# A hand-written order of all queues replaced by another, with eight PSUM banks in one pool

## The chip, the cores and the metric

The kernel runs on one core of a Trainium2 chip. The metric is device microseconds for one execution; before the change the median of three runs was 536.09 us (535.41 to 536.63). A core has five engines, each with its own queue of instructions that it works off in order: TensorE (PE in the profile, with its weight loads as PEld), VectorE (DVE), ScalarE (ACT), GpSimd (POOL) and SyncE (SP), which here issues all DMAs. Engines wait for each other through semaphores. Matmuls write to PSUM, which has eight banks; the other data lie in SBUF, and inputs and outputs in HBM.

## The reference

Two blocks follow each other. The first is a gated linear attention with a state that decays step by step; the second is an MLP with a hard-swish between its two matrices.

```python
# q, k, v, alpha: (B=4, H=8, S=768, D=48)
for t in range(S):
    state = alpha[:, :, t, :, None] * state + einsum('bhd,bhe->bhde', k[:, :, t], v[:, :, t])
    y[:, :, t] = einsum('bhd,bhde->bhe', q[:, :, t], state)
x = y.transpose(0, 2, 1, 3).reshape(3072, 384)
h = x @ w_in                              # (384, 2048)
g = h * clip(h + 3, 0, 6) / 6
out = g @ w_out                           # (2048, 384) -> (3072, 384)
```

The two weight matrices arrive as 64-bit floats and are turned into 32-bit ones on the chip. All else is 32-bit.

## The kernel before

**Attention in chunks.** The 4 x 768 tokens are cut into 24 chunks of 128 (numbered j). For a chunk, alpha, k, q and v are loaded (steps `la`, `lk`, `lq`, `lv`). For the first six chunks alpha, k and q lie in a ring of three buffers (`rings`) and are transposed by TensorE (`ta`, `tk`, `tq`, line 282); from the seventh on they are loaded in blocks and transposed by VectorE (line 286). VectorE then scans alpha backwards (`r`, line 309) and forwards (`p`, line 320) and multiplies k and q by the results (`k`, `q`, line 332). TensorE makes the scores in two halves (`sc`, line 346), which VectorE masks (`m`, line 356). k goes back to token order, by TensorE and a ScalarE copy (`kb`, `ck`, lines 374 and 378) in the first eight chunks, later by a VectorE transpose and a round trip through DRAM (`kt`, `kw`, `kr`, lines 391 to 404). TensorE makes the state update (`u`, line 429), VectorE adds it to the state (`sm`, lines 437 and 439), GpSimd decays it (`st`, line 409), and ScalarE places the state (`sv`, line 419) and q (`qa`, line 366) where the output matmuls read them. TensorE makes the chunk's output (`ya`, `yb`, line 455) and ScalarE copies it as x of the MLP (`cy`, line 464).

**Weights in slices.** There are 16 slices of 768 KB: 0 to 7 of `w_in`, 8 to 15 of `w_out`. Each is loaded (`w`, lines 162 and 166) and made 32-bit by ScalarE (`d2` line 196, `d1` line 186, for some slices `dx` line 191), VectorE (`d3`, lines 203 to 210) and, last, a GpSimd addition (`d4`, line 217).

**The MLP in groups.** A group g is two chunks, 256 tokens, so there are twelve. Groups 0 and 1 use plain matmuls for the first matrix: `fa` and `fb` (line 489) for half a group, `f` (line 478) for a whole one; the numbers after the name are the group, the slice of the weights and a bank. Group 0 uses them for the second matrix too (`b`, line 516). All other products go by schemes that need fewer matmuls and more additions: for the first matrix, 20 products `M` of four matmuls each (line 600) with sums of x (`xc`), sums of weights (`y`), copies (`n`, line 606) and output sums (`o`), where most additions are lines 537 to 541; for the second, seven products `P` of eight matmuls (line 703) with sums of the activations (`s`, lines 647 and 664), of the weights (`x`, line 647), copies (`K`, line 682) and output sums (`G`, lines 716 and 719), and a store (`O`, line 724). The activation is a ScalarE step (`fr`, `e`, line 494) and a VectorE step (`fg`, `h`, line 498). A 32-bit matmul shows as two passes in the profile (x8 is four matmuls), a transpose as one.

**Banks.** `banks` holds four PSUM tiles, t0 to t3, for attention; `bank_m` holds four others, m0 to m3, for the MLP. A step that starts a result in PSUM names its bank by a number: `sc.2.0.2` puts the two halves of the scores of chunk 2 into t0 and t2, `M.2.7.0` starts a sum of products in m0. A bank that is written again waits for its last reader.

**The order.** Nothing is planned when the kernel is built: one string lists all 1788 steps, and each step issues its instructions on its engines in that order, so the string sets all five queues. The list begins with idle matmuls (`z`, line 532, 29 in all: `z.0.5` is five of them in bank m0) mixed with the first loads.

Of the kernel before, what the change touches and what calls it, by code (L numbers as in the profile page):

```python
# [17 lines left out]
def kernel(  # L18
# [42 lines left out]
    G = 2  # L61
# [161 lines left out]
    banks = [ps.tile([C, NP * C], FP, tag=f"t{i}", name=f"t{i}_ps") for i in range(4)]  # L223
# [246 lines left out]
    bank_m = [ps.tile([C, GT * 2], FP, tag=f"m{i}", name=f"m{i}_ps") for i in range(4)]  # L470

# [278 lines left out]
    with tc.manual_schedule():  # L750
        run("""z.0.5 z.0.3 z.0.1 z.0.8 qa.0.0 w.0 d2.0 d3.0 la.0 ta.0.0 ca.0 r.0 lk.0 tk.0.1 k.0
               z.0.2 p.0 la.1 ta.1.2 lq.0 tq.0.3 ca.1 r.1 lk.1 lv.0.0 sv.0.0 d1.0 kb.0.0 ck.0 z.0.2
               u.0.2.1 sm.0.0 sv.0.1 q.0 qa.0.1 tk.1.0 k.1 p.1 z.0.2 sc.0.2.3 m.0 la.2 ta.2.0 ca.2
               dx.0 w.2 d2.2 kb.1.0 ck.1 lq.1 r.2 sm.0.1 st.1 tq.1.2 q.1 d3.2 z.0.3 d1.2 dx.2 lv.1.1
               u.1.3.1 sv.1.0 sm.1.0 p.2 sm.1.1 sc.1.0.2 m.1 ya.0.3 yb.0 cy.0 lq.2 w.1 d1.1 tq.2.1
               q.2 d4.2 lk.2 tk.2.3 k.2 fa.2.0 d4.0 st.2 sc.2.0.2 d2.1 d3.1 m.2 dx.1 d4.1 qa.1.1
               lk.3 la.3 ta.3.1 ca.3 la.4 fa.0.1 sv.1.1 w.3 r.3 ta.4.3 ca.4 r.4 tk.3.1 k.3 kb.2.0
               qa.1.0 d2.3 ya.1.2 yb.1 cy.1 fa.1.2 lq.3 ck.2 d1.3 p.3 d3.3 lv.2.2 u.2.3.2 sm.2.0
               d4.3 fb.2 tq.3.1 q.3 fb.1 qa.2.0 sm.2.1 sv.2.0 st.3 fr.0.2.0 fg.0.2 lk.4 tk.4.0
               sv.2.1 w.5 d2.5 k.4 d3.5 d1.5 qa.3.0 d4.5 qa.2.1 sc.3.1.3 m.3 w.6 d2.6 d1.6 d3.6 d4.6  # L760
               lv.3.0 lq.4 w.7 kb.3.2 fb.0 f.0.3.3 kb.4.0 ya.2.1 ck.3 u.3.3.2 sm.3.0 fr.0.3.1 fg.0.3
               fr.0.1.0 fg.0.1 qa.3.1 sv.3.0 sm.3.1 p.4 d2.7 sv.3.1 d1.7 d3.7 d4.7 f.0.5.0 fr.0.5.1
               fr.0.0.0 fg.0.5 fg.0.0 tq.4.3 ck.4 la.5 ta.5.2 f.0.6.3 ca.5 w.4 d2.4 ya.3.0 yb.3 cy.3
               fr.0.6.1 yb.2 cy.2 w.9 d2.9 q.4 qa.4.1 d1.4 d1.9 dx.4 la.6 w.8 d3.4 r.5 lk.5 w.10
               d3.9 p.5 ca.6 fg.0.6 d4.9 w.12 lq.5 lv.4.1 d2.8 d3.8 f.0.7.2 d1.8 st.4 d4.8 d4.4 w.11
               fr.0.7.0 fg.0.7 f.1.7.0 fr.1.7.1 fg.1.7 sc.4.0.2 m.4 f.1.1.1 fr.1.1.0 fg.1.1 f.1.3.3
               fr.1.3.1 d2.10 d1.10 tk.5.3 f.1.0.2 d2.12 d3.10 d4.10 w.13 fg.1.3 fr.1.0.0 fg.1.0 k.5
               d3.12 lq.6 f.1.6.0 f.1.2.1 u.4.1.0 sm.4.0 d1.12 d4.12 sv.4.0 qa.4.0 ya.4.2 fr.1.6.1
               fg.1.6 w.15 tq.5.3 fa.4.3 sv.4.1 d2.11 kb.5.1 d2.13 fr.1.2.0 f.1.4.2 fr.1.4.1 d1.11
               sm.4.1 q.5 r.6 d3.11 d3.13 fg.1.4 d4.11 lv.5.0 lk.6 tq.6 p.6 d2.15 d3.15 fg.1.2 d1.13  # L770
               d4.13 sc.5.0.3 yb.4 f.1.5.0 fr.1.5.1 fg.1.5 tk.6 m.5 b.1.0.2 fb.4 b.1.1 d1.15 d4.15
               st.5 y.5 w.14 la.7 lk.7 cy.4 d2.14 qa.5.1 ck.5 b.0.0.1 fr.0.4.0 d3.14 k.6 q.6 ca.7
               fg.0.4 d1.14 d4.14 x.0 y.1 y.10 b.0.1 y.0 y.2 u.5.2 P.1.0.0 K.1.0 qa.5.0 sv.5.0
               qa.6.1 P.1.1.3 b.0.2 b.1.2 kb.6.0 ya.5.3 y.6 s.1.0.0 sm.5.0 sv.5.1 G.1.0.0 tk.7
               s.1.1.1 s.1.2.3 x.1 yb.5 cy.5 b.1.3 sc.6.1.2 lv.6.2 ck.6 u.6.3.0 s.1.3.2 x.2 P.1.2
               b.0.3 K.1.1 y.7 s.1.4 s.1.5 y.11 y.3 r.7 xc.2.1 x.3 y.4 y.8 xc.2.3 k.7 xc.2.0 xc.2.4
               y.9 y.12 y.16 y.13 y.15 P.1.3.3 K.1.2 P.1.4 bo.1 P.1.5 xc.2.5 G.1.1.1 P.1.6 y.14 y.17
               y.19 xc.2.6 sm.6.0 G.1.2.2 y.20 M.2.0.2 lv.12.1 la.8 O.1.1 O.1.0 ca.8 y.18 y.21 y.23
               so.1 G.1.3.3 n.2.0.8 bo.0 lq.7 lv.7.0 O.1.2 m.6 xc.2.2 xc.2.10 xc.2.7 tq.7 r.8 p.7
               xc.2.8 sv.6.1 M.2.15.3 M.2.1 kb.7.3 n.2.1.9 M.2.16 M.2.2 n.2.2.10 M.2.7.0 n.2.7.11  # L780
               sm.6.1 xc.2.9 q.7 p.8 M.2.3 M.2.4 n.2.4.12 M.2.8 o.2.0.0 M.2.5 n.2.5.13 qa.7.0 sv.6.0
               st.7 lk.8 O.1.3 lq.8 lk.9 la.9 la.10 tk.8 tq.8 lq.10 lq.9 ya.6.1 yb.6 M.2.9 z.1.3
               M.2.18.1 o.2.1.0 e.2.1.1 M.2.10 cy.6 ck.7 sc.7.0.2 u.7.1.3 n.2.10.14 M.2.11 qa.7.1
               ca.9 la.11 y.22 M.2.6.2 h.2.1 q.8 m.7 e.2.0.0 h.2.0 n.2.11.15 qa.6.0 n.2.18.10 qa.8.1
               M.2.12 M.2.19 n.2.12.12 M.2.13 sm.7.0 sv.7.1 r.9 k.8 o.2.3.0 sv.7.0 ya.7.0 y.24
               o.2.5.0 n.2.13.12 o.2.2.0 yb.7 cy.7 sc.8.1.2 xc.3.1 o.2.2.1 e.2.2.1 xc.3.3 o.2.3.1
               M.2.14 xc.3.4 xc.3.0 xc.3.5 o.2.4.0 xc.3.7 xc.3.6 o.2.6.0 P.2.0.1 M.3.0.2 M.2.17
               h.2.2 o.2.6.1 e.2.3.0 h.2.3 o.2.7.0 K.2.0 n.3.0.12 M.3.1 n.3.1.9 e.2.5.1 M.3.7.0
               n.3.7.13 xc.3.8 o.2.7.1 xc.3.2 kt.8 e.2.6.0 h.2.6 tk.9 M.3.2 n.3.2.10 e.2.4.0 P.2.1.3
               h.2.4 h.2.5 s.2.0.14 e.2.7.0 G.2.0.1 h.2.7 M.3.3 M.3.4 n.3.4.8 k.9 s.2.1.11 M.3.8  # L790
               o.3.0.0 ca.10 kt.9 P.2.3.3 s.2.2.15 s.2.3.14 lv.8.2 kw.8 kr.8 lk.10 sm.7.1 xc.3.9
               M.3.5 n.3.5.11 K.2.2 e.3.0.1 xc.3.10 M.3.9 o.3.1.0 P.2.2 K.2.1 u.8.0.3 M.3.18.2 s.2.5
               M.3.10 n.3.10.14 n.3.18.15 e.3.1.0 s.2.4 P.2.4 tq.9 h.3.0 st.8 sv.8.0 M.3.11 n.3.11.8
               tk.10 p.9 sm.8.0 q.9 r.10 k.10 qa.9.0 qa.9.1 m.8 sm.8.1 h.3.1 M.3.19 o.3.5.0 kt.10
               P.2.5 G.2.2.0 st.9 M.3.12 sc.9.0.1 qa.8.0 n.3.12.10 o.3.3.0 kw.9 lv.9.0 kr.9 sv.8.1
               u.9.2.3 sm.9.0 sv.9.1 sv.9.0 G.2.1.2 sm.9.1 st.10 M.3.15.2 M.3.16 M.3.6.3 M.3.13 m.9
               o.3.4.0 o.3.6.0 tq.10 n.3.13.10 o.3.2.0 e.3.4.1 ya.8.2 yb.8 ya.9.3 yb.9 cy.9 M.3.14
               M.3.17 cy.8 xc.4.1 P.2.6 e.3.5.0 G.2.3.3 o.3.2.1 xc.4.3 h.3.4 xc.4.4 o.3.6.1 xc.4.5
               xc.4.0 xc.4.6 e.3.2.1 M.4.0.0 n.4.0.10 P.3.0.1 xc.4.7 o.3.7.0 p.10 h.3.5 o.3.3.1
               xc.4.8 M.4.7.3 M.4.1 xc.4.2 h.3.2 o.3.7.1 lk.11 O.2.2 tk.11 e.3.6.0 e.3.3.1 h.3.3  # L800
               P.3.1.2 e.3.7.1 n.4.1.13 M.4.2 K.3.0 ca.11 q.10 h.3.6 r.11 k.11 h.3.7 n.4.7.15
               lv.10.2 lv.11.0 kw.10 sc.10.0.1 kr.10 G.3.0.0 u.10.3.2 sm.10.0 qa.10.1 n.4.2.14 M.4.3
               M.4.4 M.4.8 s.3.0.9 xc.4.9 s.3.2.12 s.3.1.11 P.3.3.2 n.4.4.8 M.4.5 o.4.0.0 e.4.0.0
               sv.10.1 sm.10.1 xc.4.10 kt.11 O.2.0 O.2.3 lq.11 m.10 s.3.3.9 s.3.5 M.4.9 o.4.1.0
               P.3.2 sv.10.0 st.11 n.4.5.11 K.3.2 la.13 M.4.18.0 p.11 tq.11 lk.12 tk.12 K.3.1 M.4.10
               n.4.10.9 q.11 qa.10.0 n.4.18.12 e.4.1.1 la.12 s.3.4 ca.12 h.4.0 r.12 P.3.5 G.3.2.1
               h.4.1 M.4.11 P.3.4 n.4.11.8 M.4.12 n.4.12.14 qa.11.0 M.4.19 p.12 G.3.1.3 lq.12 kw.11
               O.2.1 tq.12 kr.11 u.11.3 sc.11.0.2 sv.11.0 O.3.1 lk.13 P.3.6 qa.11.1 M.4.6.2 G.3.3.2
               k.12 o.4.3.0 m.11 sm.11.0 sv.11.1 kt.12 M.4.13 n.4.13.14 q.12 o.4.3.1 e.4.3.0 o.4.2.0
               o.4.6.0 h.4.3 o.4.2.1 ya.10.1 ya.11.0 yb.10 yb.11 cy.11 cy.10 xc.5.1 ca.13 xc.5.3  # L810
               M.4.15.1 M.4.16 M.4.14 P.4.0.2 o.4.4.0 M.4.17 xc.5.4 o.4.5.0 xc.5.0 xc.5.5 M.5.0.0
               o.4.6.1 e.4.2.1 h.4.2 P.4.1.3 qa.12.1 e.4.4.0 xc.5.6 o.4.7.0 h.4.4 o.4.7.1 tk.13
               K.4.0 n.5.0.14 M.5.1 e.4.7.1 h.4.7 e.4.5.0 xc.5.2 h.4.5 xc.5.7 G.4.0.3 e.4.6.1 h.4.6
               s.4.1.12 s.4.0.11 xc.5.8 r.13 xc.5.9 xc.5.10 k.13 kw.12 kr.12 la.14 sc.12.2.3
               u.12.0.1 sm.12.0 n.5.1.13 M.5.2 n.5.2.15 M.5.7.1 n.5.7.8 P.4.3.3 s.4.2.9 kt.13 lk.14
               lq.13 O.3.0 O.3.3 lv.13.2 kw.13 O.4.0 lq.14 tq.13 lq.15 M.5.3 M.5.4 M.5.8 s.4.3.10
               P.4.2 sv.12.1 n.5.4.11 o.5.0.0 e.5.0.0 K.4.2 s.4.5 p.13 ca.14 M.5.9 M.5.5 n.5.5.12
               m.12 sm.12.1 o.5.1.0 q.13 P.4.5 K.4.1 G.4.2.0 qa.12.0 qa.18.0 s.4.4 h.5.0 M.5.18.0
               n.5.18.9 o.5.6.0 tk.14 qa.13.0 M.5.10 n.5.10.10 M.5.15.3 M.5.16 M.5.11 M.5.19 r.14
# [113 lines left out]
```

## Time and profile before

| What | Value |
|---|---|
| Median of three runs | 536.09 us |
| The profiled execution's span | 533.7 us |
| TensorE busy | 524.6 us, 6306 passes |
| VectorE busy | 477.2 us, 849 instructions |
| ScalarE busy | 257.2 us |
| GpSimd busy | 50.4 us, 71 instructions |
| DMA | 54.40 MB, mean 102 GB/s |
| Granted TensorE clock | 1.00 in all stages |

A row of the profile names the source line, the engine, the operation, the written tile and the tiles read, and a count. The chain of work that ended last follows the last instruction back to what released it, step by step; its rows have a start, a length and what ran. Most of it is TensorE (85%). A matmul's end is modelled in the profile, so a busy TensorE may still run slower than it could; how long a block of matmuls takes is read from the start of the next. The profiled execution's time is its span, 533.7 us, 2.4 below the median of the runs.

### The profile page before, as it was taken

To read this page: it belongs to the slowest core of one execution; us is meant where nothing else is said; L and a number is where in the kernel's file an instruction comes from. 1 tells how busy PE (TensorE), PEld (TensorE's weight loads), DVE (VectorE), ACT (ScalarE), POOL (GpSimd) and SP (SyncE) were. 2 spreads that over 40 slices of the span, in tenths; PEclk is the share of its full clock that TensorE was granted. 3 is DMA by queue.
4 is the path that set the end of the run, shared out by engine and by line. 5 is a ranking of instruction groups with operands and counts; after the bars stand their busy time and mean duration, and the time that the engine had idled before them with its cause. 6 is when DMAs were issued, how large, how long until landed. Compare 5 with 4: busy or idle time off the path is not lost.

```text
span 533.7 us, 15143 instructions
## 1 busy us (share of the span) xinstructions
PE 524.6 (98%) x6306; PEld 499.4 (94%) x6306; DVE 477.2 (89%) x849; ACT 257.2 (48%) x503; POOL 50.4 (9%) x71
## 2 busy tenths in 40 slices
PE   8799999999999999999999999999999999999997
PEld 7698886789999999999999999999999999999997
DVE  6999989999999999998999999999999899496382
ACT  3889865212653553553544444642634544553340
POOL 5333425100000000000000000000000000000000
DMA  9998876005615155254344355044454042100001
GB/s 174 217 252 256 215 216 152 21 2 154 152 30 116 32 121 135 57 140 95 87 110 113 91 124 140 19 120 102 115 136 104 11 110 43 44 2 2 15 16 37
DMA packets 124100, 54.40 MB, mean 102 GB/s; under 512 B 83328, under 2 KB 116864, under 8 KB 124032
## 3 DMA queue, kind: packets, MB, share of 16 engines
q1 hardware_dynamic: 124032, 53.44, 42.5%
q8 instruction: 49, 0.80, 0.6%
q14 instruction: 19, 0.16, 0.1%
HBM read 44.50 MB, written 8.91 MB: 100 GB/s over the span
## 4 chain that ended last, share of the span: by engine, by line
PE 85%; DVE 8%; POOL 2%; DMA 2%; ACT 1%; issue 1%; SPq 1%; DVEq 0%; POOLq 0%
PE m_ps L703 34%; PE m_ps L600 34%; PE m_ps L478 5%; PE t_ps L455 4%; PE t_ps L346 2%; PE t_ps L429 2%; PE m_ps L489 2%; PE t_ps L282 1%; DVE rings L647 1%; DMA v<-in_v_dram 1%; DVE raw L537 1%; ACT raw L191 1%; DMA kq<-in_k_dram 1%; DVE g_sb L647 1%; DVE w L537 1%
## 5 line engine op out<-in xcount | busy, mean ns | idle before, releaser
L606 ACT COPY g_sb<-m_ps 128x512 f32<-128x512 f32 x110 | 63.6, 584 | 124.9 <-PE m_ps L600 104.1
L703 PE MATMUL m_ps<-w,g_sb 128*128 128x192 f32 x704 | 121.7, 327 | 0.0
L703 PEld LDWEIGHTS m_ps<-w,g_sb 128*128 128x128 f32 x704 | 113.7, 190 | 0.4
L703 PE MATMUL m_ps<-rings,g_sb 128*128 128x192 f32 x528 | 91.5, 326 | 0.0
L703 PEld LDWEIGHTS m_ps<-rings,g_sb 128*128 128x128 f32 x528 | 85.4, 190 | 0.1
L600 PE MATMUL m_ps<-xc,w 128*128 128x128 f32 x640 | 82.7, 277 | 0.3 <-DVE w L541 0.3
L600 PEld LDWEIGHTS m_ps<-xc,w 128*128 128x128 f32 x640 | 77.5, 192 | 1.5 <-issue 0.5
L494 ACT ACTIVATE r<-g_sb,half 128x512 f32<-128x512 f32 x80 | 56.8, 722 | 32.9 <-DVE g_sb L541 12.1
L498 DVE SCALAR_TENSOR_TENSOR g_sb<-r,g_sb 128x512 f32<-128x512 f32 x80 | 53.6, 682 | 4.6 <-ACT r L494 4.2
L600 PE MATMUL m_ps<-xT,raw 128*128 128x128 f32 x400 | 52.5, 277 | 0.0
L600 PEld LDWEIGHTS m_ps<-xT,raw 128*128 128x128 f32 x400 | 48.6, 192 | 0.6
L409 POOL TENSOR_TENSOR st<-sm,R 128x192 f32<-128x192 f32 x20 | 12.9, 643 | 353.8 <-DVE sm L439 306.7
L647 DVE TENSOR_TENSOR g_sb<-g_sb 128x512 f32<-128x512 f32 (+1 forms) x55 | 42.0, 795 | 0.2
L600 PE MATMUL m_ps<-xT,w 128*128 128x128 f32 x320 | 42.0, 276 | 0.0
L600 PEld LDWEIGHTS m_ps<-xT,w 128*128 128x128 f32 x320 | 39.3, 192 | 0.1
L366 ACT COPY A<-q 48x256 f32<-48x256 f32 x88 | 35.5, 404 | 5.0 <-DVE q L332 3.7
L356 DVE TENSOR_TENSOR A<-t_ps,mask 64x256 f32<-64x256 f32 x96 | 36.0, 414 | 0.4
L478 PE MATMUL m_ps<-xT,w 128*128 128x256 f32 x144 | 32.8, 382 | 0.0
L600 PE MATMUL m_ps<-xc,raw 128*128 128x128 f32 x240 | 31.8, 276 | 0.0
L309 DVE TENSOR_TENSOR_SCAN R<-t,ones 128x516 f32<-128x516 f32 x24 | 29.7, 1236 | 1.1 <-ACT t L300 1.0
L478 PEld LDWEIGHTS m_ps<-xT,w 128*128 128x128 f32 x144 | 26.7, 190 | 3.6
L600 PEld LDWEIGHTS m_ps<-xc,raw 128*128 128x128 f32 x240 | 29.6, 192 | 0.1
(104 smaller groups left out, 731.0 us busy)
## 6 DMA issues: line engine op xcount, KB each, us to landing
raw<-in_moe_w_out_dram SPq DMA_DIRECT2D x8, 768.0 KB, 5.2
raw<-in_moe_w_in_dram SPq DMA_DIRECT2D x6, 768.0 KB, 6.8
v<-in_v_dram SPq DMA_DIRECT2D x48, 96.0 KB, 3.0
out_dram<-oh SPq DMA_DIRECT2D x44, 96.0 KB, 1.7
far<-kq SPq DMA_DIRECT2D x64, 64.0 KB, 2.2
kb<-far SPq DMA_DIRECT2D x64, 64.0 KB, 2.0
aq<-in_alpha_dram SPq DMA_DIRECT2D x36, 96.0 KB, 2.5
qq<-in_q_dram SPq DMA_DIRECT2D x36, 96.0 KB, 2.4
```

The lines of the kernel that those rows point to most:

```text
L309: nc.vector.tensor_tensor_scan(out=reverse(R, n - 1, n), data0=reverse(ax, n, n), data1=reverse(ones, n, n), initial=0.0, op0=ALU.mult, op ...
L356: nc.vector.tensor_tensor(out=to[:, a], in0=sc[a][half], in1=mask[half, half].unsqueeze(1).to_broadcast([HB, NP, HB]), op=ALU.mult)
L366: nc.scalar.copy(out=to[:, a], in_=Q_t[j][64 * a : 64 * a + D, :, half])
L409: nc.gpsimd.tensor_tensor(out=st, in0=sm, in1=R_t[j][:, :, 0:1].to_broadcast([C, NP, D]), op=ALU.mult)
L455: nc.tensor.matmul(y_of(j, (i + 1) // 2, p)[:, HB * b : HB * b + HB], vb[:, p, e : e + 32], A_t[j][:, b, 2 * p + a], start=(b == 0 and i = ...
L478: nc.tensor.matmul(h[:, f], w1[:, kk, o : o + C], xT_t[g][:, kk], start=(kk == 0), stop=(kk == KT - 1))
L494: nc.scalar.activation(out=to, in_=h, func=AF.Relu, bias=half, scale=1.0 / 6.0)
L498: nc.vector.scalar_tensor_tensor(out=to, in0=r, scalar=1.0, in1=h, op0=ALU.min, op1=ALU.mult)
L600: nc.tensor.matmul(acc[g][i][:, f * C : (f + 1) * C], spots[w][:, f * C : (f + 1) * C], x_of(g, x), start=(first and f == 0), stop=last, s ...
L606: nc.scalar.copy(out=slots[z], in_=acc[g][i])
L647: nc.vector.tensor_tensor(out=out, in0=in0, in1=in1, op=ALU.subtract)
L703: nc.tensor.matmul(to[g], a, rhs[:, f], start=(first and f == 0), stop=(last and f == HF - 1), skip_group_check=True)
```

## The change

It has two parts. One line joins the two lists of banks, so that attention's steps and the MLP's can each name any of the eight: numbers 0 to 3 are a step's own former four, 4 to 7 the other side's. And the string of steps is another one. It holds the same 1788 steps with the same counts of each kind; their order differs nearly everywhere, and so do the bank, buffer and slot numbers. What is computed and by which instruction is the same.

In the start, the first loads are those of alpha, k and q, and slice 2 of the weights is the first slice, behind v of the first chunk; before, slice 0 came first of all. The 29 idle matmuls are 8, 2, 2, 3, 1, 2, 5, 3 and 3 (before 5, 3, 1, 8, 2, 2, 2, 3 and 3). Later, the steps that hold attention's small matmuls (`sc`, `u`, `ya`, `yb`) stand next to each other more often.

```diff
     bank_m = [ps.tile([C, GT * 2], FP, tag=f"m{i}", name=f"m{i}_ps") for i in range(4)]
+    banks, bank_m = banks + bank_m, bank_m + banks
...
-        run("""z.0.5 z.0.3 z.0.1 z.0.8 qa.0.0 w.0 d2.0 d3.0 la.0 ta.0.0 ca.0 r.0 lk.0 tk.0.1 k.0
-               z.0.2 p.0 la.1 ta.1.2 lq.0 tq.0.3 ca.1 r.1 lk.1 lv.0.0 sv.0.0 d1.0 kb.0.0 ck.0 z.0.2
-               u.0.2.1 sm.0.0 sv.0.1 q.0 qa.0.1 tk.1.0 k.1 p.1 z.0.2 sc.0.2.3 m.0 la.2 ta.2.0 ca.2
...
+        run("""la.0 z.4.8 ta.0.1 ca.0 lk.0 r.0 z.1.2 tk.0.4 k.0 z.4.2 lq.0 tq.0.3 z.4.3 la.1 ta.1.4
+               p.0 lk.1 q.0 lv.0.2 w.2 z.5.1 kb.0.1 sc.0.6.5 lq.1 ca.1 tk.1.3 r.1 k.1 ck.0 u.0.7.1
+               sm.0.0 sm.0.1 z.3.2 kb.1.4 tq.1.2 la.2 m.0 qa.0.1 la.3 st.1 p.1 q.1 lv.1.0 sv.0.0
+               ya.0.3 sv.0.1 d2.2 w.1 yb.0 d1.2 dx.2 sc.1.2.7 ta.2.6 d3.2 d4.2 ta.3.5 m.1 lq.2
+               sv.1.0 ck.1 u.1.0.1 lk.2 sm.1.0 ca.2 z.2.5 sm.1.1 cy.0 ca.3 r.3 fa.2.3 lk.3 w.0
+               tq.2.3 qa.1.0 sv.1.1 lk.4 r.2 p.2 q.2 tk.2.4 k.2 qa.1.1 d2.1 ya.1.2 lq.3 d3.1 d1.1
+               dx.1 yb.1 cy.1 lv.2.2 tk.3.3 la.4 w.3 sc.2.1.6 kb.2.5 ck.2 k.3 st.2 sv.2.0 qa.0.0
...
+               o.7.6.1 u.17.4 kw.19 kr.19 e.7.0.0 n.7.5.12 u.18.5.6 ya.16.2 yb.16 sm.17.0 ya.17.0
+               G.6.2.1 sv.17.1 yb.17 o.7.3.0 sm.18.0 sm.18.1 st.19 sc.18.1.6 la.22 cy.16 cy.17
...
```

## The prediction

> **What bounds the kernel now.** I read five views: the page's busy line, busy time by stage, TensorE's waits, the chain that ended last, and the start of the timeline.
>
> ```profile
> PE 524.6 (98%) x6306; PEld 499.4 (94%) x6306; DVE 477.2 (89%) x849; ACT 257.2 (48%) x503; POOL 50.4 (9%) x71
> ```
> ```profile
> 0.00:25.00 25.00, 19.27 (x289) 16.92 (x289) 20.06 (x40) 14.91 (x21) 9.85 (x23) 1.00 1.11 198
> ...
> 200.00:250.00 50.00, 50.00 (x623) 49.37 (x616) 47.24 (x88) 22.29 (x47) 0.52 (x1) 1.00 0.43 102
> ...
> 450.00:500.00 50.00, 50.00 (x525) 49.50 (x524) 32.53 (x63) 20.27 (x41) 0.00 (x0) 1.00 0.07 18
> ```
> Columns of the second fence: stretch, its length, busy TensorE, weight load, VectorE, ScalarE, GpSimd, clock, DMA share, GB/s. TensorE is full from 25 us on. VectorE is nearly as full up to 450, then idles. The clock is 1.00.
>
> TensorE's waits after 25 us, the whole answer:
> ```profile
> PE m_ps L600 <- DVE w L541: 0.3, 1, 0.3
> PE m_ps L489 <- POOL w L217: 0.2, 1, 0.2
> PE t_ps L455 <- ACT A L366: 0.2, 1, 0.2
> ```
> So TensorE waits 0.7 us after the start. Busy TensorE can still be slow, which the chain shows:
> ```profile
> 178.39 0.89 PE m_ps L600 x8
> ...
> 259.23 0.61 PE t_ps L429 x32
> 259.84 0.48 PE t_ps L346 x32
> 260.32 1.09 PE m_ps L600 x8
> ```
> Eight passes of a product take 0.89 us, but 1.09 behind attention's small matmuls: going back to full tiles costs 0.2.
>
> The start, and two places where GpSimd's add (L217) lies beside VectorE:
> ```profile
> 0.75 0.44 SPq L162 DMA_DIRECT2D raw<-in_moe_w_in_dram  x1
> 1.25 0.47 SPq L251 DMA_DIRECT2D rings<-in_alpha_dram  x1
> ...
> 9.31 1.23 DVE L309 TENSOR_TENSOR_SCAN R<-t,ones 128x516 f32<-128x516 f32 x1 [1.02 <-ACT t L300]
> ...
> 24.90 1.60 PE m_ps L489 x12
> ...
> 81.81 2.02 POOL L217 TENSOR_TENSOR w<-raw 128x768 int32<-128x768 int32 x1 [0.17 <-POOL kq L257]
> 82.47 1.78 DVE L207 TENSOR_SCALAR w<-w 128x768 f32<-128x768 f32 x1
> ...
> 92.80 1.95 DVE L332 TENSOR_TENSOR q<-q,P 128x512 f32<-128x512 f32 x1
> ```
> The first weight slice is asked for ahead of the first alpha; the first scan starts at 9.31, the first MLP matmul at 24.90. L207 usually takes 0.70 and this form of L332 0.75, so the two holds cost 1.08 + 1.20 = 2.3 us.
>
> **Accounts.** I price TensorE by blocks without a wait (L703 16 passes 2.60, L600 8 passes 0.89, L478 12 passes 2.59, L489 12 passes 1.34, L455 128 passes 1.92, and so on). Times counts, that is 505.5 us, 6.4 of it the 29 idle matmuls. An engine's *lag* is the time at which an instruction starts less the work queued ahead of it. TensorE's lag in the trace is 1.5 at its first matmul, 12.5 after 20 us of work, 14.3 after 60, 16.5 after 120, 22.2 after 328, 25.1 at the end. With 3.1 us behind it (last output and store): 505.5 + 25.1 + 3.1 = 533.7, the span. VectorE, start to start (some 0.07 less than a row's mean), has 468.6 us of work; its lag is 4.6 at the first scan, 5.5 at 34 us. The runs' median, 536.09, is 2.4 above the span; I move that median by the span's difference.
>
> **The change, part by part.** (Lines above 470 are one higher in the changed kernel: I keep the old numbers.) All counts of work stay equal: products, adds, copies, loads, 29 idle matmuls. So only TensorE's last lag can move.
>
> *Start, VectorE.* The first alpha goes out first. In the trace the first weight slice landed at 5.6, alpha 1.2 later, each further ring load some 1.2 later; without the slice (some 2.8 us of transfer) alpha lands near 4.0. Eight idle matmuls at the slow first passes (0.213 us each, 16 of them) end at 5.0. Four transposes (0.85), the copy L300 (0.6) and hand-overs of 0.1 give a first scan at 6.6 instead of 9.31. Two weight instructions (L203, L205, 1.5 us) no longer stand ahead of it. The lag is 6.6 - 3.3 = 3.3 instead of 4.6, and some 3.5 at 34 us instead of 5.5, since no later load is due before it lands.
>
> *Start, TensorE.* The scores of chunk 2 need k.2: 21.3 of VectorE work + 3.3 = 24.6, with 16.1 of TensorE work ahead: lag 8.5. fa.1 needs slice 1: 22.7 + 3.4 + GpSimd's 1.9 = 28.0, with 18.8 ahead: 9.2. Before it was 12.5 there.
>
> *Slices later.* Slice 0 lands some 21 us later, slices 3, 5, 6, 7 some 4 to 7. Attention's matmuls cover this: slice 0 is ready at 26.3 + 3.5 + 1.9 = 31.7 and fa.0 comes at 23.8 + 9.2 = 33.0; slice 3 is ready at 39.2 and f.0.3 comes at 39.3, with no cover left. If slices come a microsecond later, that microsecond is TensorE's.
>
> *VectorE further ahead.* For each matmul that waits on VectorE, I take VectorE's work up to the producer less TensorE's work up to the matmul; TensorE's lag must exceed VectorE's by that lead. Before, the lead peaks at 7.3 (47 us of work), is 6.9 at 139 and falls to 1.9 at 322. After, it is 6.6 at 69, 9.5 at 122 (a product in bank m2, released by L537), 10.9 at 329 (scores in m2, freed by the state update L439) and 9.7 at 392. VectorE's lag beyond waits grew by 1.5 us up to 50, 4.2 up to 125, 7.7 up to 350 and 10 up to 410. Of the 2.3 of holds inside that I keep 0.6: the new order puts one add beside SBUF-only VectorE work instead of two, so between none and 1.2. Lag of VectorE: 4.6 at 60 of TensorE's work, 5.6 at 120, 9.1 at 328, 11.4 at 392. TensorE's least lag: 11.2, 15.1, 20.0, 21.1.
>
> *Fewer turns.* With eight banks, attention's small matmuls stand together: from them back to full tiles there are 28 turns after 120 us of work before, 19 after; 9 x 0.2 = 1.8 saved of the 8.6 by which the lag grew there.
>
> *End.* By the place at 122: 15.1 + 8.6 - 1.8 = 21.9. By 329: 20.0 + 2.6 = 22.6. By 392: 21.1 + 1.4 = 22.5. Hand-overs to and fro (VectorE waits for TensorE, then is waited for) add between 0 and 1.35; I take 0.3, nearest to TensorE's 0.7 us of waits. 18 more waiting instructions on TensorE at 0.02: 0 to 0.4, taken as 0, since they pass beside a running matmul. Sum 22.8 against 25.1: -2.3 us, 533.8.
>
> *A page against a row.* The row: the scan at 81.39 kept its length (1.19) beside L217, which took 2.02 instead of 1.47, while L207 and L332 were held 1.1 to 1.2. So whoever starts second pays. The Trainium skill, "GPSIMD Engine Reference", section Specifications, says that GpSimd contends with VectorE instructions in a 2-port mode or with two SBUF inputs: by it, four more of the new neighbours contend, and the sum would be some 2.2 worse.
>
> **The rivals.** Two times within 0.2% (1.07 us) are not told apart here.
> - *VectorE lighter than charged.* Part of its growth after 125 us may be hidden waiting; at half, the place at 122 alone rules: 21.5, 532.5. For it: it has gaps in just that stretch. Against: single instructions do run long.
> - *All hand-overs and a full hold are paid:* +1.05 and +0.6, 535.5. For it: leads of 9 to 11 all through, with under 1 us between what TensorE and VectorE need of each other. Against: before, the same closeness cost nothing.
> - *Contention by the four more neighbours:* 4 x 0.55 (2.02 - 1.47) = 2.2, so 536.0. For it: L217 was lengthened so. Against: GpSimd has room.
> - *Slower: VectorE's idle time lands on TensorE.* VectorE is idle 14.3 us between 100 and 450 (50 less the busy time of each stretch). Before, nobody waited for it there. In the new order it sets TensorE's pace from 100 to 420, so any idle it keeps is paid in full. It decides from 3.4 us, a quarter of it; at that quarter 537.4. For it: waits like g_sb L537 <- ACT L606 are ScalarE's. Against: most of them end on TensorE, which is late only because it is the bound.
>
> **How the numbers follow.** Forecast 0.38 (533.8; alone 532.9 to 534.9), lighter VectorE 0.17, hand-overs 0.12, contention 0.06, VectorE's idle 0.27. Faster: 0.35 + 0.17 = 0.52. Same: 0.03 + 0.11 + 0.03 + 0.03 = 0.20. Slower: 0.01 + 0.03 + 0.24 = 0.28. The range reaches from 532.0, half of the lighter case out, to 538.2, somewhat past the slower one.
>
> **What would show it.** First scan near 6.6 and first MLP matmul near 19 (start right). TensorE's waits on VectorE between 90 and 140 us, one to two microseconds in all (lead right). Fewer blocks at 1.09. L207 and L332 no longer near 1.9. Wrong, if VectorE is idle over 10 us between 100 and 420 with TensorE waiting behind it, or if slice 3 holds TensorE near 40 us.

## The result, and the profile after

The changed kernel takes 550.27 us (median of 4 runs, 549.73 to 551.68), the kernel before 535.78 us (its three runs from above and a fourth). The ratio is 1.027 with a 95% interval of 1.0256 to 1.0288: slower by 2.7%, where 533.8 us was forecast. The profiled execution has a span of 548.0 us against 533.7, so the 14.3 us between the two traces are all but 0.2 us of the difference, and the traces can be asked for it. (Lines above 470 are one higher in the changed kernel.)

The page's busy line of the changed kernel, and its busy time by stage (columns as before: stretch, length, TensorE, weight load, VectorE, ScalarE, GpSimd, clock, DMA share, GB/s):

```profile
PE 529.5 (97%) x6306; PEld 501.2 (91%) x6306; DVE 481.9 (88%) x849; ACT 257.4 (47%) x503; POOL 51.2 (9%) x71
```
```profile
0.00:25.00 25.00, 20.56 (x362) 18.63 (x362) 20.37 (x39) 15.34 (x26) 9.84 (x23) 1.00 1.12 203
200.00:250.00 50.00, 49.01 (x602) 47.55 (x601) 48.96 (x87) 23.32 (x51) 1.03 (x2) 1.00 0.36 77
450.00:500.00 50.00, 50.00 (x484) 49.70 (x483) 29.31 (x57) 19.36 (x39) 0.33 (x1) 1.00 0.05 15
```

The start gained: TensorE is busy 20.56 us of the first 25 instead of 19.27. From then on TensorE is no longer full: between 200 and 250 it does 602 passes instead of 623, and VectorE is busier than before (48.96 instead of 47.24). At 450 TensorE is full again, 14 us late. The clock is 1.00 in all stages, so the loss is not the clock's. TensorE's waits from 25 us on, which were 0.7 us in three rows before, are now 14 rows and 10.9 us, most of the loss:

```profile
PE t_ps L704 <- DVE g_sb L499: 2.4, 1, 2.4
PE m_ps L601 <- DVE g_sb L538: 1.1, 2, 0.7
PE m_ps L429 <- DMA v<-in_v_dram: 1.0, 1, 1.0
PE t_ps L282 <- DVE q L332: 1.0, 1, 1.0
PE t_ps L601 <- ACT g_sb L607: 0.8, 2, 0.5
PE m_ps L429 <- DVE oh L720: 0.8, 1, 0.8
...
PE t_ps L374 <- DVE k L332: 0.6, 1, 0.6
```

Columns: engine, written tile and line of the waiting group, what released it, us in total, times, the longest. But for the first, no row is long; 7.6 of the 10.9 us end on VectorE, at six of its lines. Such a list says that VectorE is behind everywhere, not why. The chain that ended last now also passes from engine to engine. Around 394 us it shows a product of the second bank at the plain price, and one behind a wait at more:

```profile
393.90 0.49 ACT g_sb L607
394.39 0.04 issue
394.44 1.16 PE m_ps L601 x8
395.60 0.89 PE t_ps L601 x8
```

**Lags.** With the account of the prediction (an instruction's start less the work queued ahead of it), TensorE's lag in us is:

| TensorE's work | 20 | 60 | 80 | 100 | 200 | 300 | 340 | 360 | 400 | 500 |
|---|---|---|---|---|---|---|---|---|---|---|
| before | 12.5 | 14.3 | 15.3 | 15.8 | 19.0 | 21.2 | 22.4 | 22.9 | 23.6 | 25.1 |
| changed | 11.0 | 13.1 | 14.5 | 17.6 | 23.0 | 29.4 | 31.6 | 35.4 | 37.6 | 39.4 |

The start keeps 1.5 us of gain at 20, 0.7 at 80; then 15 us go, steadily, with a step of 3.8 between 340 and 360.

**Where VectorE's time goes.** Its single instructions are not slower: form by form, between 100 and 350 us, they sum to 1.1 us less than in the kernel before. What differs is how they follow each other. Rows of the changed kernel's timeline (start, length, what ran):

```profile
6.76 1.23 DVE L309 TENSOR_TENSOR_SCAN R<-t,ones 128x516 f32<-128x516 f32 x1 [2.57 <-ACT t L300]
8.02 0.18 DVE L313 RECIPROCAL t<-R 128x4 f32<-128x4 f32 x1
8.12 0.66 DVE L332 TENSOR_TENSOR k<-m_ps,R 128x512 f32<-128x512 f32 x1
...
190.14 0.34 DVE L439 TENSOR_TENSOR s<-m_ps,st 128x192 f32<-128x192 f32 x1
190.59 0.36 DVE L439 TENSOR_TENSOR sm<-m_ps,s 128x192 f32<-128x192 f32 x1
190.86 0.68 DVE L499 SCALAR_TENSOR_TENSOR g_sb<-r,g_sb 128x512 f32<-128x512 f32 x1
```

The reciprocal needs the scan directly in front of it: the scan ends at 7.99, it starts at 8.02. The multiplication behind it needs the scan too, but not the reciprocal: it starts at 8.12, 0.08 *before* the reciprocal's end at 8.20. So with the second state update (190.59, 0.11 behind the end of the first at 190.48) and the multiplication after it (190.86, 0.09 before its end). Over all instructions between 100 and 350 us the medians are +0.035 for the 73 that wait only for the VectorE instruction directly in front, +0.104 for the seven that also wait for TensorE, and -0.081 for the 157 that wait for nothing. (Those that wait for an instruction further back on VectorE start as these do: -0.08 as well, 18 of them between 100 and 430 us that wait for the one before the last.) I call two such instructions a *pair*; a pair costs VectorE 0.12 us, 0.19 in the second case. The built programs can be counted: 83 pairs in the kernel before, 183 in the changed one. From 100 to 430 us it is 32 against 111, 3.9 us against 14.5. That is theory A. Theory B was late transfers and waits for other engines, theory C longer single instructions.

### The profile page after: what moved, and what is told of

It is laid out like the page before. It is cut to its first block, busy times and chain, and to the rows that moved or that the text cites. A ratio compares the mean times of both kernels' runs of the same rounds, so it can differ in the third digit from the quotient of the medians.

```text
span 548.0 us, 15084 instructions
## 1 busy us (share of the span) xinstructions
PE 529.5 (97%) x6306; PEld 501.2 (91%) x6306; DVE 481.9 (88%) x849; ACT 257.4 (47%) x503; POOL 51.2 (9%) x71
## 5 line engine op out<-in xcount | busy, mean ns | idle before, releaser
L704 PE MATMUL t_ps<-rings,g_sb 128*128 128x192 f32 x384 | 66.7, 327 | 0.1
L704 PE MATMUL t_ps<-w,g_sb 128*128 128x192 f32 x352 | 61.1, 327 | 2.4 <-DVE g_sb L499 2.4
L704 PEld LDWEIGHTS t_ps<-rings,g_sb 128*128 128x128 f32 x384 | 62.3, 190 | 0.8 <-DVE rings L648 0.3
L704 PE MATMUL m_ps<-w,g_sb 128*128 128x192 f32 x352 | 61.3, 327 | 0.7 <-DVE g_sb L648 0.4
L704 PEld LDWEIGHTS t_ps<-w,g_sb 128*128 128x128 f32 x352 | 56.9, 190 | 2.8 <-DVE g_sb L499 2.7
L704 PEld LDWEIGHTS m_ps<-w,g_sb 128*128 128x128 f32 x352 | 57.0, 190 | 1.4 <-DVE g_sb L499 0.6
L601 PE MATMUL m_ps<-xc,w 128*128 128x128 f32 x360 | 47.6, 278 | 1.7 <-DVE g_sb L538 1.1
L601 PEld LDWEIGHTS m_ps<-xc,w 128*128 128x128 f32 x360 | 43.9, 192 | 2.5 <-DVE g_sb L538 1.4
L366 ACT COPY A<-q 48x256 f32<-48x256 f32 x88 | 35.4, 403 | 16.1 <-DVE q L332 13.8
L601 PE MATMUL t_ps<-xc,w 128*128 128x128 f32 x280 | 38.2, 280 | 0.8 <-DVE g_sb L538 0.4
L601 PEld LDWEIGHTS t_ps<-xc,w 128*128 128x128 f32 x280 | 34.3, 191 | 2.5 <-DVE g_sb L538 1.1
L601 PE MATMUL t_ps<-xT,raw 128*128 128x128 f32 x240 | 31.6, 277 | 0.5 <-ACT g_sb L607 0.5
```

The source lines that it names most:

```text
L366: nc.scalar.copy(out=to[:, a], in_=Q_t[j][64 * a : 64 * a + D, :, half])
L601: nc.tensor.matmul(acc[g][i][:, f * C : (f + 1) * C], spots[w][:, f * C : (f + 1) * C], x_of(g, x), start=(first and f == 0), stop=last, s ...
L704: nc.tensor.matmul(to[g], a, rhs[:, f], start=(first and f == 0), stop=(last and f == HF - 1), skip_group_check=True)
```

## The experiments

**Pairs taken apart, half of them, none, and brought together.** Four kernels in which VectorE's queue alone is another; the queues of the other four engines, all counts and all banks stay. In the first, one of the moves is:

```diff
-  e.3.6.0 n.4.0.15 h.3.6 xc.4.8 xc.4.9 sm.10.0 P.3.1.6
+  e.3.6.0 n.4.0.15 h.3.6 xc.4.8 sm.10.0 xc.4.9 P.3.1.6
```

(`xc.4.9` no longer stands directly behind `xc.4.8`.)

> The changed kernel with VectorE's queue alone rearranged: 117 of its steps stand elsewhere, so that instructions which wait for the VectorE instruction directly in front of them fall from 183 to 53; the queues of TensorE, ScalarE, GpSimd and SyncE, all counts, banks and buffers stay as in the changed kernel. Theory A (such a pair costs VectorE 0.12 us, since the second one starts 0.035 us after the end of the first instead of 0.082 us ahead of it, and in the new order VectorE sets TensorE's pace): 130 pairs are 15.6 us of VectorE's time, of which what lies before 430 us and behind no other wait reaches the end: 8 to 12 us faster than the changed kernel, 538 to 542. Theory B (the loss is transfers that come late and shared banks, that is, waits for other engines): unchanged within 1.5 us, near 550. Theory C (VectorE's single instructions run longer beside other engines): unchanged within 1 us.

Measured 544.3 us, ratio to before 1.0166 (1.0137 to 1.0195): 6.0 faster than the changed kernel, less than the 8 to 12 expected, far more than theories B and C allow. The same state update as above, in this kernel's timeline:

```profile
185.72 0.35 DVE L439 TENSOR_TENSOR s<-m_ps,st 128x192 f32<-128x192 f32 x1
185.99 0.68 DVE L542 SCALAR_TENSOR_TENSOR g_sb<-t_ps,g_sb 128x512 f32<-128x512 f32 x1
186.59 0.28 DVE L538 TENSOR_TENSOR xc<-xT 128x128 f32<-128x128 f32 x1
186.79 0.68 DVE L538 TENSOR_TENSOR g_sb<-t_ps,g_sb 128x512 f32<-128x512 f32 x1
187.39 0.34 DVE L439 TENSOR_TENSOR sm<-m_ps,s 128x192 f32<-128x192 f32 x1
```

Every row starts 0.08 before the end of the row above it; the second L439 has three others between itself and the first, and no gap. Pairs between 100 and 430 us cost 2.1 us now instead of 14.5, but the waits of VectorE that the profile lists there rose from 5.0 to 12.5: over half of what was saved is spent waiting.

> The changed kernel with half as many pairs separated: 183 become 118 by moving 60 VectorE steps, the other four queues unchanged. Theory A: about half of what 130 pairs bring, 4 to 6 us faster than the changed kernel, near 545. Theories B and C: unchanged within 1.5 us.

Measured 546.82 us (1.0200, 1.0169 to 1.0232): 3.5 faster, where 4 to 6 were expected. Pairs cost 8.6 us between 100 and 430. TensorE stood (was idle, waiting) 1.65 and 0.99 us near 100 us, and its granted clock was 0.93 from 100 to 150: its lag at 100 us of work is 3.5 above the changed kernel's, while from there to 500 it grows by 16.6 instead of 21.8.

> The changed kernel with as many VectorE steps moved (117) as in the first of these runs, each by up to three places, and the number of pairs left at 183; the other four queues unchanged. Theory A: unchanged within 1 us, near 550. If moving steps by itself helps (results earlier or later for their readers, and not the pairs): faster by several microseconds, as the first run.

Measured 556.93 us (1.0407, 1.0384 to 1.0430): 6.7 *slower* than the changed kernel, which neither guess allowed. Its rows by stage and its timeline show what happened at one place:

```profile
50.00:75.00 25.00, 25.00 (x131) 22.34 (x130) 24.43 (x37) 17.68 (x26) 10.57 (x8) 1.00 0.76 218
75.00:100.00 25.00, 21.52 (x209) 16.81 (x208) 24.34 (x35) 14.48 (x25) 10.52 (x11) 0.80 0.70 181
```
```profile
80.56 0.66 PE L374 MATMUL t_ps<-ident,k 128*128 128x128 f32 x4 [0.80 <-DVE g_sb L499]
83.90 1.12 PE L374 MATMUL m_ps<-ident,k 128*128 128x128 f32 x4 [2.69 <-DVE g_sb L499]
```

TensorE stood 0.80 and 2.69 us within 4 us, and then worked at a mean clock of 0.80 up to 100 (twelve passes of L479 took 2.75 us at 74.43 and 4.63 us at 89.76). Its lag went from 13.0 at 60 us of work to 21.9 at 80, 7.4 above the changed kernel; from 80 to 500 it grew by 23.2, there by 24.8. With the pairs taken apart it grew by about 19.8. So with the pairs kept, moving 117 steps brought 1.6 us from 80 us on, against 5 us with the pairs gone, much as theory A says; the loss lies at one place, two stands with a slower clock behind them. As a control the run is therefore good only for the stretch behind that place.

> The kernel before with VectorE's queue alone rearranged the other way: 103 steps moved so that pairs rise from 83 to 200; the other four queues, banks and buffers stay as before. Theory A: 117 pairs are 14 us of VectorE's time; VectorE had up to some 5 us of room, so 7 to 11 us slower than before, 543 to 547. Theories B and C: unchanged within 1.5 us, near 536.

Measured 546.76 us (1.0207, 1.0191 to 1.0222): 11.0 slower than before, at the upper end of what theory A gave. 2.4 of it is there at 20 us of TensorE's work (clock 0.94 up to 25 us and 0.93 from 25 to 50); from 100 to 480 its lag grows by 18.2 instead of 9.4, where the changed kernel's grows by 21.8. So pairs alone slow the old order by much of what the change cost, with the same banks, the same transfers and the same order on four engines. It does not follow that they are as much of the loss in the new order; there, taking them apart brought 6.0.

**Late loads.** In the changed kernel VectorE stood for one alpha, and TensorE behind it (VectorE's waits from 100 to 450 us, then the timeline):

```profile
DVE t L286 <- DMA aq<-in_alpha_dram: 2.7, 1, 2.7
```
```profile
373.61 1.10 DVE L286 STREAM_TRANSPOSE t<-aq 128x512 f32<-128x512 f32 x1 [2.66 <-DMA aq<-in_alpha_dram]
...
377.02 1.57 PE L704 MATMUL t_ps<-w,g_sb 128*128 128x192 f32 x8 [2.36 <-DVE g_sb L499]
```

This load stood in SyncE's queue behind the reading back of k of an earlier chunk (`kr.19`), which waited there, once the k that it reads had been written, for a state update on TensorE to release its buffer (in the changed kernel from 354.4 to 357.1), and behind four other loads (`la.22`, `lv.19`, `lq.20`, `lv.23`).

```diff
-  u.17.4 kw.19 kr.19 e.7.0.0
+  u.17.4 kw.19 la.21 kr.19 e.7.0.0
...
-  yb.18 lv.23.1 la.21 xc.8.6
+  yb.18 lv.23.1 xc.8.6
```

> The changed kernel with one step of SyncE's queue moved: the load of alpha of chunk 21 stands ahead of the reading back of k of chunk 19, which waits there for TensorE, instead of behind it and three other loads; the queues of the other four engines are unchanged. In the changed kernel VectorE stood 2.66 us for this alpha at 373.6, and TensorE 2.5 us behind that, at 377. Theory A alone (only the pairs count): unchanged within 1 us, near 550, since the stand would move elsewhere. Theory B for this place (a late load is paid in full, because VectorE has nothing spare): 2 to 3 us faster than the changed kernel, near 547.7.

Measured 547.25 us (1.0232, 1.0207 to 1.0257), 3.0 faster than the changed kernel. The step of the lag between 340 and 360 is gone (31.7 to 32.7), elsewhere the curve grows as before within 0.3. TensorE's longest wait is no longer there:

```profile
PE m_ps L601 <- DVE g_sb L538: 1.3, 2, 0.7
PE t_ps L282 <- DVE q L332: 1.0, 1, 1.0
```

> The kernel with VectorE's pairs separated (54 left), and two loads moved forward in SyncE's queue: alpha of chunk 21 ahead of the reading back of k of chunk 19, and k of chunk 13 ahead of the reading back of k of chunk 12; nothing else. There VectorE stood 2.70 us for the alpha at 369.5 and 1.92 us for k at 235.8, and TensorE 2.87 and 1.52 us behind these. If both stands go and nothing takes their place: 4 us faster than with the pairs separated alone, near 540. If the time given back by the pairs is simply taken by waits wherever VectorE gets ahead: less than 1.5 us faster, 543 or more.

The edit is the one above and `lk.13` moved ahead of `kr.12`. Measured 541.61 us in the median (1.0109, 1.0075 to 1.0144), its runs from 539.06 to 543.66; the profiled execution has 537.3. So 2.7 faster than with the pairs apart in the median, less than the 4 expected, and 5.4 between the profiles, because the profiled execution is the fastest of the four; why its runs lie so wide apart is open. Its trace shows both stands gone and nothing in their place: TensorE's lag is 28.7 at the end instead of 34.2.

**VectorE's work cut.** The forward scan covers a quarter of its columns:

```diff
+    nc.vector.memset(Ps, 1.0)
...
-            out=P_t[j], data0=aX[j % 2][:, 0:n], data1=ini[j % 2], initial=0.0,
+            out=P_t[j][:, 0:W], data0=aX[j % 2][:, 0:W], data1=ini[j % 2][:, 0:W], initial=0.0,
```

> The changed kernel with VectorE's work cut: the forward scan covers 129 columns of 516, the rest of its result stays 1.0, so the attention's output is another one; 24 scans get some 0.87 us shorter, 19 us less for VectorE up to 430 us. The order of all queues is unchanged. If VectorE sets TensorE's pace in the changed kernel: 8 to 13 us faster than it, 537 to 542. If TensorE's own time or the transfers set it: unchanged within 2 us, near 549.

Measured 544.43 us (1.0161, 1.0134 to 1.0188): 5.8 faster, not 8 to 13. With 19 us less to do VectorE has room again (47.20 us busy between 200 and 250 instead of 48.96), and TensorE still waits 7.6 us after 25 us: 4.1 on VectorE, 2.1 on loads, 1.0 on ScalarE. I take these waits for chains in which TensorE, ScalarE and VectorE hand one result on and the next matmul stands close behind; no run separates them.

> The kernel before with the same cut in VectorE's forward scans (19 us less up to 430 us, the attention's output is another one), its order unchanged. If TensorE sets the pace there, as its 0.7 us of waits say: 0 to 2 us faster than before, 534 to 536. If VectorE set it there as well: 8 us faster or more.

Measured 534.81 us (0.9985, 0.9975 to 0.9994): 0.8 faster, as expected for a kernel whose pace TensorE sets. The same cut is worth seven times as much in the changed order. TensorE's waits after 25 us in this run, the whole answer (lines one higher):

```profile
PE t_ps L456 <- ACT A L367: 0.2, 1, 0.2
```

**Orders searched anew.** For these, steps are cut so that other work can stand between a pair:

```diff
+    def inverse(j):
+        ic = ini[j % 2]
         nc.vector.reciprocal(out=ic.rearrange("r (p w) -> r p w", w=W)[:, :, 0:1],
...
-        "d1": round_low, "d2": magnitude, "dx": sign, "d3": high_bits, "d4": add_low,
+        "d1": round_low, "d2": magnitude, "dx": sign, "d3": lambda i: high_bits(i, 0), "d5": lambda i: high_bits(i, 1),
+        "d6": lambda i: high_bits(i, 2), "d4": add_low,
```

> The same instructions in an order searched anew from the changed kernel with its pairs separated and the two loads moved, all five queues now: it counts 0.117 us for every VectorE instruction that waits for the one directly in front of it, and the step of the backward scan is cut into the scan and the reciprocal, that of the weights into its two or three instructions, and a sum of activations in two, so that other work can stand between; 3 pairs are left of 183. If pairs, late loads and VectorE's stands are the whole of what the changed kernel lost, TensorE is left with its own 505.5 us, a start of 10 to 12, turns of 4 to 6 and an end of 3: 525 to 531 in all. If something else is lost in orders of this kind: 535 or more.

Measured 543.14 us (1.0140, 1.0123 to 1.0157); expected 525 to 531. In its trace (of the slowest of the four runs) the loss is all in the first 125 us: TensorE's lag is 13.8 at 20 us of work and 25.7 at 100, with a stand of 3.27 us that ends at 117.7 and a clock of 0.93 from 100 to 150. From 100 to 500 the lag grows by 9.1, as little as in the kernel before.

> The same search from the kernel before, with its banks in two groups and its order of the start kept where nothing is gained by another: pairs fall from 83 to 4. VectorE had few microseconds on the end there, so what is to be had is mostly TensorE's turns and the start: 527 to 533. If the pairs matter nowhere but where VectorE sets the pace: 533 to 536.

Measured 540.01 us (1.0090, 1.0057 to 1.0123); expected 527 to 533. Again the start (14.5 instead of 12.5 at 20 us of work, clock 0.85 up to 25 us and 0.95 from 25 to 50), and 1.37 us at 271 in which TensorE stood without a wait that the profile shows. I take it that my costs for the crowded loads of the start were too low, so that a search that moves them is led astray; no run shows this by itself. Hence the last two, with the first 72 us kept:

> The kernel with pairs separated and two loads moved, its first 72 us (TensorE's first 55 us of work) left as they are, and all five queues behind that in an order searched anew, which counts 0.117 us for a pair, 0.12 us for each change between kinds of matmul tiles, and DMAs up to 1.2 us later than their usual landing; the steps of the scan, the weights and one sum are cut so that other work stands between. 29 pairs are left. If the loss of the changed kernel was pairs, late loads and hand-overs, TensorE's lag is 14 after 80 us of work as there and grows by no more than the 9.4 of the kernel before: 24 at the end, a span of 532 to 533, 0.2 to 0.6% faster than the kernel before. If what slowed the freely searched orders lies in such orders as such and not in their start: 538 or more.

Measured 535.42 us (0.9991, 0.9983 to 1.0000): no measurable difference from the kernel before, and 14.9 us faster than the changed kernel, with its banks and, but for VectorE's queue, its start; behind that, the order is another one on all five queues. The lag is 13.4 at 80 and 25.2 at the end (expected 24). The expected 0.2 to 0.6% is not reached: TensorE stands 0.64, 0.70, 0.45 and 0.90 us at 97, 118, 123 and 189, the last without a wait that the profile shows.

> The same search from the kernel before, its first 72 us left as they are: 27 pairs of 83 are left. TensorE's lag is 15.2 after 80 us of work as before. If VectorE's pairs and hand-overs cost that kernel nothing, as its 0.7 us of waits say, only turns between tile kinds are to be had, 0 to 2 us: 533.5 to 536. A gain of over 2 us would say that VectorE held TensorE up there in ways that its waits do not show.

Measured 534.79 us (0.9986, 0.9977 to 0.9995): 0.8 faster than before, the best version here, though by less than the 0.2% that a single comparison can tell. TensorE waits after 25 us as little as before (the whole answer; lines one to four higher):

```profile
PE m_ps L493 <- POOL w L218: 0.2, 1, 0.2
PE t_ps L459 <- ACT A L370: 0.2, 1, 0.2
```

So 56 pairs fewer were worth 0.8 us at most where TensorE sets the pace, and 130 fewer were worth 6 us where VectorE does.

**The sum.** By the medians: 550.3 changed, 544.3 with the pairs apart, 541.6 with two loads earlier as well, 535.4 with the order behind 72 us searched anew, 535.6 before. So 6.0 us go with the pairs, 2.7 with the late loads, and 6.2 with what the search mended. The 2.7 alone is not clear of the noise (1.0137 to 1.0195 against 1.0075 to 1.0144), but the four runs with one load moved by itself (547.08 to 549.66) all lie below those of the changed kernel. By the spans of the profiled executions (548.0, 542.7, 537.3, 533.8, 533.7) it is 5.3, 5.4 and 3.5: the second and third shares differ because the profiled execution with the loads moved was the fastest of its four. What the last share is, hand-overs between engines or other things, no run separates. The three are not independent either: in the changed kernel one load alone was worth 3.0 us, and VectorE's other waits grew when its pairs were gone.

## Why the prediction was wrong

The sum 505.5 + lag + 3.1 holds: 505.5 + 39.4 + 3.1 is 548.0. The lag at the end was put at 22.8 (by its own terms 22.6 + 0.3, so 22.9).

- *Start, VectorE: right.* First scan at 6.76 (6.6 forecast), lag 3.5 at 5 us of work (3.3). But 3.5 was to last up to 34 us; at 30 us of VectorE's work it was 5.9, before 5.5. 25 pairs in the first 50 us against 17 are a part of it, and waits for TensorE such as the 0.5 us in front of the row at 33.74.
- *Start, TensorE: the right sign, half the size.* First MLP matmul at 20.83 (near 19; before 24.90), lag 11.0 at 20 us of work (9.2; before 12.5). The gain of 3.3 was 1.5, and 0.7 at 80.
- *Slices later: right.* Where slice 3 was due, at 42.3, TensorE waited 0.19 us, and for VectorE; the slice had been ready since 41.6. The cover just held.
- *VectorE further ahead: right to 2 us, and to 0.5 at the first three places.* Take the lag of VectorE that the trace shows at the producer, add my lead, and compare with the lag that TensorE had there:

| TensorE's work | lead forecast | VectorE's lag, forecast | measured | sum of lead and measured | TensorE's lag, measured |
|---|---|---|---|---|---|
| 69 | 6.6 | 4.6 | 6.7 | 13.3 | 13.6 |
| 122 | 9.5 | 5.6 | 9.0 | 18.5 | 18.0 |
| 329 | 10.9 | 9.1 | 20.0 | 30.9 | 31.1 |
| 392 | 9.7 | 11.4 | 28.8 | 38.5 | 36.5 |

In the kernel with pairs apart and loads moved the third row is 13.6 + 10.9 = 24.5, measured 24.2. So the rule by which VectorE's lag turns into TensorE's held, and what went into it did not.

- *VectorE's lag of 4.6, 5.6, 9.1, 11.4: the step that failed.* I took its growth "beyond waits" from the trace of before and carried it over, as if it were a property of the instructions. It was a property of their neighbours: 32 pairs between 100 and 430 us there, 111 in the new order. With pairs apart and loads moved the lag at 329 is 13.6: these two are 6.4 of the 10.9 by which 9.1 was too low there, and the other 4.5 stay open. The late alpha of chunk 21, 2.7 us at the last place, had no term at all: of the loads, the prediction weighed only the slices and those of the start. That the lag at 329 is the same 20.0 in both traces is chance: before, it was waiting that nobody paid for; after, it is largely pairs, and the lead of 10.9 puts TensorE that far behind it. The number of pairs could have been counted in the two programs before any run, and its price stood in the trace of before, in the scan of 9.31, which ended at 10.54, and its reciprocal:

```profile
10.57 0.18 DVE L313 RECIPROCAL t<-R 128x4 f32<-128x4 f32 x1
10.67 0.66 DVE L332 TENSOR_TENSOR k<-t_ps,R 128x512 f32<-128x512 f32 x1
```

- *Fewer turns: too much.* 28 turns to full tiles became 19 between 100 and 480 us of TensorE's work, as counted, which with the turns to small ones saves 1.9 us (0.12 and 0.09 us each). But attention's groups now follow each other, and from one kind of small tile to another costs about 0.12 as well (L429 to L455 and L455 to L346, 11 times instead of once): some 1.2 back. Net some 0.7, forecast 1.8. The Trainium skill, "TensorEngine Tiling", section Key Properties, says that a change of tiling mode drains TensorE; it gives no time, and the trace agrees with the rule, for these small ones too: the first matmul after the change starts 0.149 us behind the last one before it, where between L346 and L429 it is 0.038.
- *Holds by GpSimd: right, and better.* VectorE's instructions that run over 0.3 us longer than their form's median sum to 3.5 us before and 0.3 after. L207 and L332 near 1.9 are gone. (Their usual lengths are 0.60 and 0.68; the 0.70 and 0.75 of the prediction were means with the two long ones in them.) The rival of contention by four more neighbours, 2.2 us, is out. The Trainium skill, "GPSIMD Engine Reference", section Specifications, says that GpSimd contends with VectorE instructions that read two SBUF inputs; in the changed kernel it is almost always GpSimd that pays, which has room (L217 takes 2.27 us at 77.36 beside a scan that keeps its 1.22).
- *VectorE lighter than charged*, and *all hand-overs*: both rested on the same lag of VectorE and fall with it.
- *Slower, VectorE's idle time lands on TensorE:* the right side, and its mechanism in part. The sign named for it was there: VectorE idle 11.0 us between 100 and 420, TensorE waiting behind it. But it was idle as long in the kernel before (11.1). Of the 11.0 us, 5.0 are waits that the profile lists, 2.7 of them the late alpha, and 5.1 lie between pairs, which hold VectorE's queue by themselves. What stays when pairs and late loads are gone, 3.6 us by the traces and 6.1 by the medians, is above the 3.4 from which this rival was to decide; whether it is this mechanism is not shown.
- *Signs named beforehand:* TensorE's waits on VectorE between 90 and 140 us were to be one to two us, "lead right". They were there (1.0 us in two rows between 88 and 145), but the price of a VectorE that rules was not in them.

## What to carry to other kernels

When a change of order puts an engine in front that had room before, its own time has to be counted anew in the new order, neighbour by neighbour: list for each engine the instructions that wait for the one directly in front of them, and price them by rows of the old trace. An engine with room hid such costs here, and loads that are just in time as well; here the new order put TensorE's matmuls closer behind VectorE, and more of them were paid. Where a search over orders is led by costs, keep what the costs don't describe well (here the first 72 us) as it was measured.

## What was not expected of the hardware

- A VectorE instruction that waits only for the VectorE instruction directly in front of it starts 0.035 us after its end (73 of them between 100 and 350 us); one that waits for nothing, or for a VectorE instruction further back, starts in the median 0.08 us ahead of the end of its forerunner. The 0.035 us is the same for all forms that stand in front, from a 0.18 us reciprocal to a 1.2 us scan. The Trainium skill, "VectorE: DVE Perf Modes", section "The DRAIN you can't avoid", reports that a semaphore after each operation costs nothing extra. Here the wait of the next instruction on it costs 0.12 us; 130 such waits fewer went with 6.0 us of the kernel's time, and 117 more with 11.0.
- Two stands of TensorE of 0.80 and 2.69 us within 4 us were followed by a mean granted clock of 0.80 from 75 to 100 us, 1.65 and 0.99 us by 0.93 from 100 to 150, and one of 3.27 us also by 0.93 from 100 to 150; a single stand of 2.36 us at 377 was not followed by any. A stand can cost twice its length: behind the 3.5 us of the first case the lag was 7.4 us above the changed kernel's.
- Changes between TensorE's tile kinds cost 0.12 us to full tiles, 0.09 from them, and 0.12 between some of attention's kinds: a first full matmul starts 0.148 us behind the last small one, against 0.038 between two kinds that cost nothing, and a first small one 0.205 us behind L600, whose own matmuls are 0.112 apart.
